# Loading the first q and v in head halves, and the first weights in row halves, in a fused attention and FFN kernel

## The chip, the cores and the metric

The kernel runs on one core of a Trainium2 chip. The metric is device time in microseconds (us), of one execution of the whole program; a time is the median of several executions. A "landing" is the moment at which the last of the sixteen parts of a transfer reports; landing times of single transfers were read from the trace's semaphore updates.

## The reference

Linear attention (softmax of q over the head dimension, of k over the sequence), then a gated FFN, for 8 batches of 576 rows, 8 heads of 64, and 512 → 1536 → 512 columns:

```python
q_s = softmax(q, axis=-1); k_s = softmax(k, axis=2)          # [8, 8, 576, 64] each
kv  = np.einsum('bhsd,bhse->bhde', k_s, v)
x   = np.einsum('bhsd,bhde->bhse', q_s, kv)                  # then to [4608, 512]
out = (gelu(x @ w_gate) * (x @ w_val)) @ w_out
```

## The kernel before

All matmuls are in fp16 and inputs arrive in f32, so every input passes through an exp or a cast. Batch 0's attention has to be done before the FFN can start; until then TensorE runs warm-up matmuls that nobody reads. Every load is issued by SyncE, in this order: q, k, v of batch 0, then the weights by column chunks. One call of `load` is two transfers, for the even and the odd SBUF rows:

```python
    WCH = [0, 128, 256] + list(range(512, F + 1, 256))     # weight column chunks
    wstp = ctx.enter_context(tc.tile_pool(name="wstp", bufs=6))   # staging buffers
    def load(src, nm, b, h0, h1, n0):
        tiles[(nm, b)] = ld_b[nm][b % len(ld_b[nm])]
        for t, c0 in ((0, n0), (1, 1)):
            nc.sync.dma_start(
                out=tiles[(nm, b)][t:P:2, h0:h1, c0 * D:NC * D],
                in_=src[b, h0:h1].rearrange("h (m n) d -> m h (n d)", n=NT)[...])
    # ... cut ...
    for src, nm, n0 in ((q, "q", 1), (k, "k", 0), (v, "v", 0)):
        load(src, nm, 0, 0, H, n0)
    for c in range(NW):
        load_w_gv(c)                       # one gate and one value chunk
    # ... cut ...
    exp("q", 0, 0, 4, 1); exp("q", 0, 4, 8, 1)        # ScalarE
    exp("k", 0, 0, 4);    exp("k", 0, 4, 8)
    warm_pe(35)
    norm(0, 0, "dve", 1); norm(0, 1, "pool", 1)       # head pairs 0 to 3
    norm(0, 2, "dve", 1); norm(0, 3, "pool", 1)
    unit_t(0, 0, "dve")                               # transposes of q, copy on VectorE
    warm_pe(9)
    cast_v(0, 0, 4, "dve"); cast_v(0, 4, 6, "act")
    unit_t(0, 1, "act")
    cast_v(0, 6, 8, "dve")
    # ... cut: loads of batches 1 and 2 ...
    warm_pe(2)
    unit_kv(0, 0); unit_kv(0, 1)                      # k^T v, lower and upper heads
    # ... cut: x, then ffn_first over two column tiles ...
```

The softmax here doesn't subtract the row's maximum and nothing guards it: scores larger than these inputs give would overflow.

Of the kernel before, what the change touches and what calls it, by code (L numbers as in the profile page):

```python
# [9 lines left out]
f32 = mybir.dt.float32  # L10
f16 = mybir.dt.float16
# [7 lines left out]
def kernel(  # L19
# [10 lines left out]
    nc = tc.nc  # L30
# [15 lines left out]
    VW = D + 1  # L46
    WCH = [0, 128, 256] + list(range(512, F + 1, 256))
    NW = len(WCH) - 1
# [15 lines left out]
    warm = const.tile([P, 512], f16)  # L64
    nc.vector.memset(warm, 0.0)
    ident = const.tile([P, P], f16)
    make_identity(nc, ident)
    mask = const.tile([P, 2, D], f32)
    nc.vector.memset(mask, 0.0)
    nc.vector.memset(mask[0:64, 0, :], 1.0)  # L70
    nc.vector.memset(mask[64:128, 1, :], 1.0)
    tiny = const.tile([P, 80], f32)
    nc.vector.memset(tiny, 0.0)
    ek_b, eq_b, v16_b = [], [], []
    for i in range(2):
        ek_b.append(const.tile([P, NC, C], f16, name=f"ek{i}"))
        eq_b.append(const.tile([P, NC, C], f16, name=f"eq{i}"))
        v16_i = const.tile([P, NC, H, VW + 1], f16, name=f"v16_{i}")
        nc.gpsimd.memset(v16_i[:, :, :, D:D + 1], 1.0)
        v16_b.append(v16_i)  # L80
    xtr = const.tile([P, HP, B * REM], f16)
    q0r = const.tile([64, H, D], f32)
    eq0r = const.tile([P, C], f16)
    nc.vector.memset(eq0r[64:128, :], 1.0)

    ld_b = {}
    for nm, n, fill in (("k", 2, -1e30), ("v", 1, 0.0), ("q", 2, 0.0)):
        ld_b[nm] = []
        for i in range(n):
            t = const.tile([P, H, NC * D], f32, name=f"{nm}t{i}")  # L90
            (nc.vector if i == 0 else nc.gpsimd).memset(t[:, :, 0:D], fill)
            ld_b[nm].append(t)

# [30 lines left out]
    def copy_on(eng, dst, src):  # L124
        if eng == "pool":
            nc.gpsimd.tensor_copy(out=dst, in_=src)  # L126
        elif eng == "act":
            nc.scalar.copy(out=dst, in_=src)  # L128
        else:
            nc.vector.tensor_copy(out=dst, in_=src)  # L130

    def cast_w(nm, c, eng="pool"):
# [42 lines left out]
    def norm(b, hp, eng="dve", n0=0):  # L175
        norm_sum(b, hp, n0)
        norm_mul(b, hp, eng)
# [41 lines left out]
    def unit_t(b, g, eng="dve"):  # L219
        eqt = get_eqt(b)  # L220
        pst = ps_att.tile([P, 2, MAIN], f16, name="pst", tag="att")
        for j in range(2):
            hp = 2 * g + j
            for n in range(NM):
                nc.tensor.transpose(  # L225
                    pst[:, j, n * P:(n + 1) * P],
                    eq_b[b % 2][:, n + 1, hp * P:(hp + 1) * P], ident)
        copy_on(eng, eqt[:, 2 * g:2 * g + 2, 0:MAIN], pst)

# [56 lines left out]
    def unit_xrem(b, eng="act"):  # L286
# [4 lines left out]
        copy_on(eng, xtr[:, :, b * REM:(b + 1) * REM], psx)  # L291

    def warm_pe(n):
        ps = ps_big.tile([P, 512], f32, name="pswarm", tag="mm")
        for _ in range(n):
            nc.tensor.matmul(ps, ident, warm, start=True, stop=True)  # L296
# [25 lines left out]
    def ffn_first(xt, after):  # L322
# [14 lines left out]
        for fi, (psg, psv) in enumerate(ps):  # L337
            mm_gv(psg, wg_sb, xt, fi, [3])
            mm_gv(psv, wv_sb, xt, fi, [3])
            hts.append(gate(psg, psv))  # L340
        return hts

# [61 lines left out]

    for src, nm, n0 in ((q, "q", 1), (k, "k", 0), (v, "v", 0)):
        load(src, nm, 0, 0, H, n0)
    for c in range(NW):
        load_w_gv(c)
    for c in range(3):
        load_w_o(c)  # L410
    load(q, "q", 1, 0, H, 0)
    for c in range(3, NO):
# [8 lines left out]
    exp("q", 0, 4, 8, 1)  # L421
    exp("k", 0, 0, 4)
    exp("k", 0, 4, 8)
    warm_pe(35)
    norm(0, 0, "dve", 1)
    norm(0, 1, "pool", 1)
    norm(0, 2, "dve", 1)
    norm(0, 3, "pool", 1)
    unit_t(0, 0, "dve")
    warm_pe(9)  # L430
    cast_v(0, 0, 4, "dve")
    cast_v(0, 4, 6, "act")
    unit_t(0, 1, "act")
    cast_v(0, 6, 8, "dve")
    for h0 in (0, 4):
# [3 lines left out]
    nc.sync.dma_start(out=q0r, in_=q[0].rearrange("h (m n) d -> m h (n d)", n=NT)[:, :, 0:D])  # L439
    warm_pe(2)  # L440
    unit_kv(0, 0)
    unit_kv(0, 1)
    cast_w("wg", 0, "pool")
    cast_w("wv", 0, "pool")
    unit_x(0, 0, "act", True)
    unit_x(0, 1, "act", True)
    unit_x(0, 2, "dve", True)
    unit_x(0, 3, "act", True)
    preload(ACTF.Gelu)
    for c in range(1, NW):  # L450
        cast_w("wg", c)
        cast_w("wv", c)
# [7 lines left out]
    def at(b, kind, i, *fns):  # L460
# [3 lines left out]

    at(0, FI, NFI - 1, L(exp, "q", 1), L(exp, "k", 1, 0, 4),
       L(cast_w_o, 3), L(cast_w_o, 4), L(cast_w_o, 5),
       L(norm, 1, 0), L(norm, 1, 1, "pool"), L(norm_sum, 1, 2), L(norm_mul, 1, 2, "pool"),
       L(cast_v, 1, 0, 4, "act"), L(exp, "k", 1, 4, 8))
# [6 lines left out]
              [L(unit_x, 1, 3, "dve")]]  # L475
    first = {0: [[], []], 1: first1}

# [53 lines left out]
    for b in order:  # L531
        xt = get_xt(b) if b < B else xtr
        hts = []
        fi0 = 0
        if b in first:
            hts = ffn_first(xt, first[b])
            fi0 = len(hts)
            ride(b, FI, fi0 - 1)
# [57 lines left out]
```

## Time and profile before

| | before |
|---|---|
| time, median | 321.69 us |
| span of the profiled execution | 319.8 us |
| q landed (two transfers) | 5.09, 6.35 |
| k landed | 8.17, 9.96 |
| v landed | 11.61, 12.93 |
| first kv matmul | 14.60 |
| first gate matmul of the FFN | 17.20 |
| third gate tile | 20.78 |

Read it from below. From the third gate tile on TensorE works at a fixed pace, so a microsecond there is a microsecond of the whole. It is late because a chain of transfers and element-wise work comes first. The lines of the profile that show this are in the prediction.

### The profile page before, as it was taken

To read this page: it belongs to the slowest core of one execution; us is meant where nothing else is said; L and a number is where in the kernel's file an instruction comes from. 1 tells how busy PE (TensorE), PEld (TensorE's weight loads), DVE (VectorE), ACT (ScalarE), POOL (GpSimd) and SP (SyncE) were. 2 spreads that over 40 slices of the span, in tenths; PEclk is the share of its full clock that TensorE was granted. 3 is DMA by queue.
4 is the path that set the end of the run, shared out by engine and by line. 5 is a ranking of instruction groups with operands and counts; after the bars stand their busy time and mean duration, and the time that the engine had idled before them with its cause. 6 is when DMAs were issued, how large, how long until landed. Compare 5 with 4: busy or idle time off the path is not lost.

```text
span 319.8 us, 4482 instructions
## 1 busy us (share of the span) xinstructions
PE 314.4 (98%) x1650; PEld 149.5 (47%) x1650; DVE 194.7 (61%) x343; ACT 140.0 (44%) x178; POOL 44.5 (14%) x60
## 2 busy tenths in 40 slices
PE   8999999999999999999999999999999999999995
PEld 3544454445445444544444444444444444444443
DVE  3944366498889578846794679457952444233431
ACT  3563564898352563246423743384321233103300
POOL 2567460340002000120003000300000000000000
PEclk9999999999999999999999999999999999999999
DMA  6999999940187216821492039302011110040002
GB/s 230 367 383 395 400 389 385 394 148 0 68 291 250 54 66 210 321 62 66 124 383 81 29 124 373 121 21 119 14 55 29 68 66 0 16 108 10 0 34 99
DMA packets 42342, 50.76 MB, mean 159 GB/s; under 512 B 3408, under 2 KB 38096, under 8 KB 42320
## 3 DMA queue, kind: packets, MB, share of 16 engines
q1 hardware_dynamic: 42176, 50.41, 45.6%
q8 instruction: 13, 0.21, 0.3%
q14 instruction: 9, 0.07, 0.1%
q10 hardware_dynamic: 144, 0.07, 0.1%
HBM read 37.75 MB, written 9.44 MB: 148 GB/s over the span
## 4 chain that ended last, share of the span: by engine, by line
PE 96%; ACT 1%; issue 1%; DVE 1%; POOL 0%; POOLq 0%; ACTq 0%
PE psg L304 28%; PE psy L348 28%; PE psv L304 28%; PE pswarm L296 4%; PE pskv L199 3%; PE psx L282 2%; PE pst L225 1%; PE psl L369 1%; DVE kv_sb L207 0%; ACT L309 0%; ACT L148 0%; PE psxr L289 0%; ACT eq L148 0%; PE pstr L237 0%; ACT gl L309 0%
## 5 line engine op out<-in xcount | busy, mean ns | idle before, releaser
L309 ACT ACTIVATE gl<-psg 128x512 f32<-128x512 f32 x108 | 63.9, 598 | 127.3 <-PE psg L304 125.5
L311 DVE SCALAR_TENSOR_TENSOR ht<-psv,gl 128x512 f16<-128x512 f32 x108 | 72.9, 682 | 64.7 <-PE psv L304 63.2
L304 PE MATMUL psg<-xt,wg_sb 128*128 128x512 f16 x384 | 100.6, 379 | 0.2
L304 PE MATMUL psv<-xt,wv_sb 128*128 128x512 f16 x384 | 100.2, 379 | 0.0
L348 PE MATMUL psy<-wo_sb,ht 128*128 128x512 f16 x420 | 95.5, 379 | 0.0
L304 PEld LDWEIGHTS <-wv_sb 128*128 128x128 f16 x432 | 42.2, 98 | 51.5 <-issue 0.9
L304 PEld LDWEIGHTS <-wg_sb 128*128 128x128 f16 x432 | 41.5, 98 | 47.6 <-issue 0.8
L348 PEld LDWEIGHTS <-ht 128*128 128x128 f16 x420 | 40.4, 98 | 47.2 <-DVE ht L311 0.2
L397 DVE TENSOR_SCALAR yo<-psy 128x512 f32<-128x512 f32 x30 | 20.6, 689 | 31.0 <-PE psy L348 31.0
L126 POOL CAST v<-vt 128x640 f16<-128x640 f32 x26 | 18.3, 743 | 140.1 <-DMA vt<-in_v_dram 122.9
L165 DVE TENSOR_REDUCE rq<-eq 128x10 f32<-128x640 f16 (+1 forms) x32 | 25.4, 792 | 9.3 <-ACT eq L148 8.9
L172 DVE TENSOR_TENSOR eq<-eq,rrq 128x640 f16<-128x640 f16 (+1 forms) x28 | 22.9, 817 | 0.3
L148 ACT ACTIVATE ek<-kt 128x1280 f16<-128x1280 f32 (+1 forms) x11 | 19.1, 1746 | 3.0 <-DVE rrq L167 1.6
L148 ACT ACTIVATE eq<-qt 128x2560 f16<-128x2560 f32 (+1 forms) x9 | 18.3, 2049 | 4.3 <-DMA qt<-in_q_dram 4.2
L248 DVE STREAM_TRANSPOSE et<-eq 128x640 f16<-128x640 f16 x20 | 16.9, 845 | 0.7
L128 ACT CAST xt<-psx 128x512 f16<-128x512 f32 x17 | 9.2, 588 | 15.9 <-PE psx L282 15.9
L296 PE MATMUL pswarm<-warm,ident 128*128 128x512 f16 x46 | 12.3, 430 | 1.4 <-POOL ident masks.py:199 1.4
L304 PE MATMUL psg<-xtr,wg_sb 128*128 128x512 f16 x48 | 12.3, 379 | 0.0
L304 PE MATMUL psv<-xtr,wv_sb 128*128 128x512 f16 x48 | 12.3, 379 | 0.0
L199 PEld LDWEIGHTS <-ek 128*128 128x128 f16 x160 | 10.3, 97 | 3.6 <-issue 0.4
L199 PE MATMUL pskv<-v,ek 128*128 128x130 f16 x160 | 11.8, 220 | 0.0
L130 DVE CAST xt<-psx 128x512 f16<-128x512 f32 x15 | 9.7, 682 | 1.8 <-PE psx L282 1.8
(59 smaller groups left out, 129.4 us busy)
## 6 DMA issues: line engine op xcount, KB each, us to landing
out_dram<-yo SPq DMA_DIRECT2D x14, 512.0 KB, 3.5
qt<-in_q_dram SPq DMA_DIRECT2D x9, 512.0 KB, 6.7
kt<-in_k_dram SPq DMA_DIRECT2D x7, 640.0 KB, 7.4
vt<-in_v_dram SPq DMA_DIRECT2D x7, 640.0 KB, 7.9
qt<-in_q_dram SPq DMA_DIRECT2D x7, 640.0 KB, 6.1
kt<-in_k_dram SPq DMA_DIRECT2D x7, 512.0 KB, 8.0
vt<-in_v_dram SPq DMA_DIRECT2D x7, 512.0 KB, 8.5
eqt<-et SPq DMA_DIRECT2D x80, 40.0 KB, 1.9
```

The costliest lines, as they stand in the source:

```text
L126: nc.gpsimd.tensor_copy(out=dst, in_=src)
L148: nc.scalar.activation(out=dst[:, n0:NC, h0 * D:h1 * D].rearrange("p n (h d) -> p h n d", d=D), in_=tiles[(nm, b)][:, h0:h1, n0 * D:NC * D ...
L165: nc.vector.reduce_sum(rq, e, axis=mybir.AxisListType.X)
L172: (nc.gpsimd if eng == "pool" else nc.vector).tensor_tensor(out=e, in0=e, in1=rrq.unsqueeze(-1).to_broadcast((P, n, 2, D)), op=ALU.mult)
L199: nc.tensor.matmul(pskv[:, j, :], ek_b[b % 2][:, n, hp * P:(hp + 1) * P], v16_b[b % 2][:, n, 2 * hp:2 * hp + 2, 0:VW], start=(n == 0), sto ...
L248: nc.vector.transpose(out=et[:, :, hp].rearrange("p c (n i) -> p n c i", i=32), in_=eq_b[b % 2][:, :, hp * P:(hp + 1) * P].rearrange("p n ...
L296: nc.tensor.matmul(ps, ident, warm, start=True, stop=True)
L304: nc.tensor.matmul(ps, w[:, ci, fi * P:(fi + 1) * P], xt[:, ci, :], start=(ci == 0), stop=(ci == HP - 1))
L309: nc.scalar.activation(out=gl, in_=psg, func=ACTF.Gelu)
L311: nc.vector.scalar_tensor_tensor(out=ht, in0=psv, scalar=_H_SCALE, in1=gl, op0=ALU.mult, op1=ALU.mult)
L348: nc.tensor.matmul(psy, hts[fi][:, ns * P:(ns + 1) * P], wo_sb[:, fi, :], start=(fi == 0), stop=(fi == NFI - 1))
L397: nc.vector.tensor_scalar(out=yo, in0=psy, scalar1=1.0 / _H_SCALE, scalar2=None, op0=ALU.mult)
```

## The change

The intent is to start that chain on half of the data. q and v come in head halves, so that the lower four heads are complete earlier; the first 256 weight columns come in row halves, as the lower rows are all that the lower heads' x needs; and the first two column tiles of gate and value run on the lower half while kv and x of the upper heads are still being made. Around it VectorE takes one multiply from GpSimd, ScalarE takes the first transpose copy ahead of k's exp, GpSimd takes the cast of v's last two heads from VectorE, VectorE takes the second transpose copy from ScalarE, and the memsets that k's and v's loads wait for go first. Cut to its core:

```diff
-    WCH = [0, 128, 256] + list(range(512, F + 1, 256))
+    WCH = [256, 384, 512] + list(range(768, F + 1, 256))
+    def load_w_rows(half):          # 256 columns, half of the rows; a staging tile per transfer
+        for w, nm in ((moe_w_gate, "wg"), (moe_w_val, "wv")):
+            t = wst_tile(f"{nm}st", 2, WCH[0])
+            nc.sync.dma_start(out=t, in_=...[:, 2 * half:2 * half + 2, 0:WCH[0]])
-    for src, nm, n0 in ((q, "q", 1), (k, "k", 0), (v, "v", 0)):
-        load(src, nm, 0, 0, H, n0)
+    load(q, "q", 0, 0, 4, 1)
+    load(q, "q", 0, 4, 8, 1)
+    load(k, "k", 0, 0, H, 0)
+    load(v, "v", 0, 0, 4, 0)
+    load(v, "v", 0, 4, 8, 0)
+    for half in range(2):
+        load_w_rows(half)
...
-    norm(0, 3, "pool", 1)
-    unit_t(0, 0, "dve")
+    norm(0, 3, "dve", 1)
+    unit_t(0, 0, "act")             # ahead of k's exps
+    exp("k", 0, 0, 4)
+    exp("k", 0, 4, 8)
...
     unit_kv(0, 0)
+    unit_x(0, 0, "dve", True)
+    unit_x(0, 1, "act", True)
+    unit_kv(0, 1)                   # ffn_first0 then runs two tiles on the lower half first
```

Cut: the order of memsets, the `ffn_first0` function, one warm-up bank for all warm-ups, q of batch 1 in two halves and one of its multiplies on VectorE.

More of the change, by code (lines that the diff above doesn't have):

```diff
@@ L64 @@
     warm = const.tile([P, 512], f16)
-    nc.vector.memset(warm, 0.0)
     ident = const.tile([P, P], f16)
-    make_identity(nc, ident)
     mask = const.tile([P, 2, D], f32)
-    nc.vector.memset(mask, 0.0)
-    nc.vector.memset(mask[0:64, 0, :], 1.0)
-    nc.vector.memset(mask[64:128, 1, :], 1.0)
     tiny = const.tile([P, 80], f32)
-    nc.vector.memset(tiny, 0.0)
     ek_b, eq_b, v16_b = [], [], []
@@ L77 @@
         eq_b.append(const.tile([P, NC, C], f16, name=f"eq{i}"))
-        v16_i = const.tile([P, NC, H, VW + 1], f16, name=f"v16_{i}")
-        nc.gpsimd.memset(v16_i[:, :, :, D:D + 1], 1.0)
-        v16_b.append(v16_i)
+        v16_b.append(const.tile([P, NC, H, VW + 1], f16, name=f"v16_{i}"))
     xtr = const.tile([P, HP, B * REM], f16)
@@ L83 @@
     eq0r = const.tile([P, C], f16)
-    nc.vector.memset(eq0r[64:128, :], 1.0)
-    ld_b = {}
-    for nm, n, fill in (("k", 2, -1e30), ("v", 1, 0.0), ("q", 2, 0.0)):
-        ld_b[nm] = []
-        for i in range(n):
-            t = const.tile([P, H, NC * D], f32, name=f"{nm}t{i}")
-            (nc.vector if i == 0 else nc.gpsimd).memset(t[:, :, 0:D], fill)
-            ld_b[nm].append(t)
+    ld_b = {nm: [const.tile([P, H, NC * D], f32, name=f"{nm}t{i}") for i in range(n)]
+            for nm, n in (("k", 2), ("v", 1), ("q", 2))}
+    nc.vector.memset(warm, 0.0)
+    nc.vector.memset(ld_b["k"][0][:, :, 0:D], -1e30)
+    nc.vector.memset(ld_b["v"][0][:, :, 0:D], 0.0)
+    nc.vector.memset(tiny, 0.0)
+    nc.vector.memset(mask, 0.0)
+    nc.vector.memset(mask[0:64, 0, :], 1.0)
+    nc.vector.memset(mask[64:128, 1, :], 1.0)
+    nc.vector.memset(eq0r[64:128, :], 1.0)
+    nc.vector.memset(ld_b["q"][0][:, :, 0:D], 0.0)
+    make_identity(nc, ident)
+    for i in range(2):
+        nc.gpsimd.memset(v16_b[i][:, :, :, D:D + 1], 1.0)
+    nc.gpsimd.memset(ld_b["k"][1][:, :, 0:D], -1e30)
+    nc.gpsimd.memset(ld_b["q"][1][:, :, 0:D], 0.0)
     wg_sb = wpool.tile([P, HP, F], f16, name="wg_sb")
@@ L130, in copy_on, with cast_w_rows @@
             nc.vector.tensor_copy(out=dst, in_=src)
+    def load_w_rows(half):
+        for w, nm in ((moe_w_gate, "wg"), (moe_w_val, "wv")):
+            t = wst_tile(f"{nm}st", 2, WCH[0])
+            nc.sync.dma_start(
+                out=t, in_=w.rearrange("(ci p) f -> p ci f", p=P)[
+                    :, 2 * half:2 * half + 2, 0:WCH[0]])
+            wst[(nm, "rows", half)] = t
+    def cast_w_rows(nm, half, eng="pool"):
+        dst = (wg_sb if nm == "wg" else wv_sb)[:, 2 * half:2 * half + 2, 0:WCH[0]]
+        copy_on(eng, dst, wst[(nm, "rows", half)])
     def cast_w(nm, c, eng="pool"):
@@ L227, in unit_t @@
                     eq_b[b % 2][:, n + 1, hp * P:(hp + 1) * P], ident)
-        copy_on(eng, eqt[:, 2 * g:2 * g + 2, 0:MAIN], pst)
+        st["evac_t"] = lambda eng: copy_on(eng, eqt[:, 2 * g:2 * g + 2, 0:MAIN], pst)
+        if eng != "none":
+            st["evac_t"](eng)
     def unit_trem(b):
@@ L291, in unit_xrem @@
         copy_on(eng, xtr[:, :, b * REM:(b + 1) * REM], psx)
+    pswarm = ps_big.tile([P, 512], f32, name="pswarm", tag="mm")
     def warm_pe(n):
-        ps = ps_big.tile([P, 512], f32, name="pswarm", tag="mm")
+        ps = pswarm
         for _ in range(n):
@@ L340, in ffn_first, with ffn_first0 @@
             hts.append(gate(psg, psv))
+        return hts
+    def ffn_first0(xt, after):
+        ps = {}
+        for fi in range(2):
+            for nm in ("g", "v"):
+                ps[(nm, fi)] = ps_big.tile([P, 512], f32, name="ps" + nm, tag="mm")
+        for nm, w in (("g", wg_sb), ("v", wv_sb)):
+            for ci in range(2):
+                for fi in range(2):
+                    mm_gv(ps[(nm, fi)], w, xt, fi, [ci])
+            after.pop(0)()
+        for nm, w in (("g", wg_sb), ("v", wv_sb)):
+            for fi in range(2):
+                mm_gv(ps[(nm, fi)], w, xt, fi, [2])
+        hts = []
+        for fi in range(2):
+            for nm, w in (("g", wg_sb), ("v", wv_sb)):
+                mm_gv(ps[(nm, fi)], w, xt, fi, [3])
+            hts.append(gate(ps[("g", fi)], ps[("v", fi)]))
         return hts
@@ L410 @@
         load_w_o(c)
-    load(q, "q", 1, 0, H, 0)
+    load(q, "q", 1, 0, 4, 0)
+    load(q, "q", 1, 4, 8, 0)
     for c in range(3, NO):
@@ L421 @@
     exp("q", 0, 4, 8, 1)
-    exp("k", 0, 0, 4)
-    exp("k", 0, 4, 8)
-    warm_pe(35)
     norm(0, 0, "dve", 1)
@@ L427 @@
     norm(0, 2, "dve", 1)
-    norm(0, 3, "pool", 1)
-    unit_t(0, 0, "dve")
-    warm_pe(9)
+    norm(0, 3, "dve", 1)
+    warm_pe(29)
+    unit_t(0, 0, "act")
+    exp("k", 0, 0, 4)
+    exp("k", 0, 4, 8)
+    warm_pe(8)
+    unit_t(0, 1, "none")
     cast_v(0, 0, 4, "dve")
+    st["evac_t"]("dve")
     cast_v(0, 4, 6, "act")
-    unit_t(0, 1, "act")
-    cast_v(0, 6, 8, "dve")
+    cast_v(0, 6, 8, "pool")
+    warm_pe(2)
+    for half in range(2):
+        cast_w_rows("wg", half)
+        cast_w_rows("wv", half)
+    unit_kv(0, 0)
+    warm_pe(2)
+    unit_x(0, 0, "dve", True)
+    unit_x(0, 1, "act", True)
+    warm_pe(1)
+    unit_kv(0, 1)
+    preload(ACTF.Gelu)
     for h0 in (0, 4):
@@ L439 @@
     nc.sync.dma_start(out=q0r, in_=q[0].rearrange("h (m n) d -> m h (n d)", n=NT)[:, :, 0:D])
-    warm_pe(2)
-    unit_kv(0, 0)
-    unit_kv(0, 1)
-    cast_w("wg", 0, "pool")
-    cast_w("wv", 0, "pool")
-    unit_x(0, 0, "act", True)
-    unit_x(0, 1, "act", True)
-    unit_x(0, 2, "dve", True)
-    unit_x(0, 3, "act", True)
-    preload(ACTF.Gelu)
-    for c in range(1, NW):
+    for c in range(NW):
         cast_w("wg", c)
@@ L463 @@
     L = lambda f, *a: (lambda: f(*a))
-    at(0, FI, NFI - 1, L(exp, "q", 1), L(exp, "k", 1, 0, 4),
+    at(0, FI, NFI - 1, L(exp, "q", 1, 0, 4), L(exp, "q", 1, 4, 8), L(exp, "k", 1, 0, 4),
        L(cast_w_o, 3), L(cast_w_o, 4), L(cast_w_o, 5),
-       L(norm, 1, 0), L(norm, 1, 1, "pool"), L(norm_sum, 1, 2), L(norm_mul, 1, 2, "pool"),
+       L(norm, 1, 0), L(norm, 1, 1), L(norm_sum, 1, 2), L(norm_mul, 1, 2, "pool"),
        L(cast_v, 1, 0, 4, "act"), L(exp, "k", 1, 4, 8))
@@ L475 @@
               [L(unit_x, 1, 3, "dve")]]
-    first = {0: [[], []], 1: first1}
+    first0 = [L(unit_x, 0, 2, "act"), L(unit_x, 0, 3, "dve")]
     at(1, FI, 2, L(unit_trem, 1))
@@ L534 @@
         fi0 = 0
-        if b in first:
-            hts = ffn_first(xt, first[b])
+        if b < 2:
+            hts = ffn_first0(xt, first0) if b == 0 else ffn_first(xt, first1)
             fi0 = len(hts)
```

## The prediction

> **What bounds the kernel now.** I read the page's busy table and clock row first, then the chain of waits, then the timeline of each engine over the first 21 us, because the change touches only the start.
>
> ```profile
> PE 314.4 (98%) x1650; PEld 149.5 (47%) x1650; DVE 194.7 (61%) x343; ACT 140.0 (44%) x178; POOL 44.5 (14%) x60
> PEclk9999999999999999999999999999999999999999
> PE 96%; ACT 1%; issue 1%; DVE 1%; POOL 0%; POOLq 0%; ACTq 0%
> ```
>
> TensorE is busy for 98% of the span, at full granted clock, and is 96% of the chain that ended last. But part of that is warm-up, matmuls whose result nobody reads. The timeline of TensorE shows which:
>
> ```profile
> 1.36 9.65 PE L296 MATMUL pswarm<-warm,ident 128*128 128x512 f16 x35 [1.36 <-POOL ident masks.py:199]
> 10.85 0.82 PE L225 MATMUL pst<-ident,eq 128*128 128x128 f16 x8
> 11.50 2.10 PE L296 MATMUL pswarm<-warm,ident 128*128 128x512 f16 x9
> 13.44 0.79 PE L225 MATMUL pst<-ident,eq 128*128 128x128 f16 x8
> 14.07 0.59 PE L296 MATMUL pswarm<-warm,ident 128*128 128x512 f16 x2
> 14.60 1.46 PE L199 MATMUL pskv<-v,ek 128*128 128x130 f16 x20
> 15.99 1.37 PE L282 MATMUL psx<-eqt,kv_sb 128*128 128x512 f16 x4
> 17.20 0.72 PE L304 MATMUL psg<-xt,wg_sb 128*128 128x512 f16 x2
> 20.78 1.03 PE L304 MATMUL psg<-xt,wg_sb 128*128 128x512 f16 x4
> 21.64 1.03 PE L304 MATMUL psv<-xt,wv_sb 128*128 128x512 f16 x4
> ```
>
> The kv matmuls start at 14.60, the first gate matmul at 17.20, the third gate tile (column tile 2) at 20.78, and from there four matmuls take 21.64 - 20.78 = 0.86 us, again and again. So 20.78 is the mark to watch: all that follows is TensorE work at a fixed pace, and the end moves with it. From 20.78 on I find, in the starts of successive matmuls, 1.4 us of pauses in all, most of them at the seam to batch 1 (46 to 65 us) and each behind work that TensorE itself released. The gain can only be what the start gives. What sets 14.60 and 17.20 is in the timelines of the other engines (VectorE, ScalarE, GpSimd in this order):
>
> ```profile
> 7.53 0.69 DVE L165 TENSOR_REDUCE rq<-eq 128x8 f32<-128x512 f16 x1 [3.35 <-ACT eq L148]
> 10.84 0.92 DVE L172 TENSOR_TENSOR eq<-eq,rrq 128x512 f16<-128x512 f16 x1
> 12.51 0.64 DVE L130 COPY eqt<-pst 128x1024 f16<-128x1024 f16 x1
> 13.06 2.21 DVE L130 CAST v<-vt 128x1280 f16<-128x1280 f32 x2
> 15.38 0.17 DVE L204 RECIPROCAL rck<-pskv 128x2 f32<-128x2 f32 x1
> 6.44 2.00 ACT L148 ACTIVATE eq<-qt 128x1024 f16<-128x1024 f32 x2 [4.20 <-DMA qt<-in_q_dram]
> 10.07 2.43 ACT L148 ACTIVATE ek<-kt 128x1280 f16<-128x1280 f32 x2 [1.63 <-DVE rrq L167]
> 12.73 1.04 POOL L172 TENSOR_TENSOR eq<-eq,rrq 128x512 f16<-128x512 f16 x1 [1.52 <-DVE rrq L167]
> 13.74 1.18 POOL L126 CAST wg_sb<-wgst 128x512 f16<-128x512 f32 x1
> 15.69 0.61 POOL L126 CAST wg_sb<-wgst 128x512 f16<-128x512 f32 x1
> ```
>
> ScalarE waits for q until 6.44, VectorE starts on its first sum at 7.53 and is then occupied without a gap until after 15. It is the path: q, exp, norms, one transpose copy, v casts, kv. Single transfers' landing times in the trace: q 5.09 and 6.35, k 8.17 and 9.96, v 11.61 and 12.93, the first weight chunks 13.69 (gate) and 14.49 (value).
>
> **What the Trainium skill says.** "TensorE: Matmul & The Clock Gate", section "Back-to-back issue gap", gives N / 2.4 + 2.5 ns for a warm matmul, 216 ns at 512 columns; the trace agrees (0.86 us for four). "GPSIMD Engine Reference", section "1. Specifications", says that GpSimd's SBUF interfaces are shared with VectorE, with contention against VectorE instructions in a two-port mode or with two SBUF inputs. The trace agrees: the cast at 13.74, beside the v cast, took 1.18 us and the same form at 15.69 took 0.61; the two-input multiply on VectorE at 10.84, beside GpSimd's multiply at 10.17, took 0.92 where the earlier one at 8.48, with GpSimd idle, took 0.69. "VectorE: DVE Perf Modes", section "Mode 2×_2P — use both read ports for one tensor", lets a single-source SBUF copy run at two elements per cycle, f32 included. No uncontended cast of v is in this trace; I come back to it. "DMA: Bandwidth & Descriptors", section "Specifications", asks for at least 512 B for line rate. Here both the 512 B weight rows and the 1 KB rows arrive at 344 to 395 GB/s, so I expect little from the longer rows.
>
> **The change part by part.** The bytes ahead of any given point are unchanged: q, k, v, then 1 MB of weights (row halves of 256 columns in place of two 128-column chunks), so the DMA stream, which is saturated, gives nothing. Only what has to have landed before work starts is smaller.
>
> 1. q in head halves. The lower heads are complete when half of q is, about 5.2 (half the bytes by the first landing of 5.09), against 6.35. The first exp takes half of 2.00, 1.04 with its start. So VectorE's first sum starts at about 5.3 + 1.04 + 0.05 = 6.4, not 7.53: 1.1 us earlier.
>
> 2. Norms. VectorE now multiplies for pairs 0, 2 and 3; GpSimd keeps pair 1. Step by step (sum 0.69, reciprocal 0.20, multiply 0.69, all from the rows before, starts overlapping a little): sum 0 6.4, multiply 0 7.35 to 8.05, sum 1 to 8.65, reciprocal to 8.85, sum 2 to 9.4, multiply 2 (beside GpSimd, 0.92) to 10.6, sum 3 to 11.2, multiply 3 to 12.15. Before, the last sum ended at 12.35 and GpSimd's multiply at 13.77; so the fourth pair is 1.6 us earlier though VectorE does one multiply more.
>
> 3. The first transpose copy moves to ScalarE (a 128x1024 copy there took 1.01 at 14.27) ahead of k's exp. TensorE is ready after 29 warm-ups at about 9.5, GpSimd's multiply ends near 10.0, so the copy runs 10.45 to 11.5, the k exps to 12.75 and 14.0, the v cast of heads 4, 5 to 14.75. Before, the k exps were done at 12.50. This is later but the lower half needs only 12.75.
>
> 4. Casting the lower v. Half of v has landed at about 11.45 (9.96 plus half of the 2.97 to 12.93), VectorE is free at 12.2. The cast of 128x1280 took 1.40 before with GpSimd beside it all the time. Now GpSimd stands still until v's upper half lands at 12.95. At one element per cycle it would again take 1.4 (sum rows of 640 take 0.82, of 512 take 0.69, which puts the fixed part at 0.17, and 1280 at 1.5); that it took less, contended, suggests the double rate, which is 0.67 + 0.17 = 0.84. So the lower kv matmuls start between 13.2 and 13.75, not at 14.60.
>
> 5. From kv to the third tile. Before, kv start to first x was 15.99 - 14.60 = 1.39 us (ten matmuls, reciprocal, the masked multiply). Then: x 0 and 1 at 14.6 and 14.85 (fast cast) or 15.1 and 15.4 (slow), the copies of x take 0.43 to begin and 0.69, so x tile 0 is in SBUF at 15.7 or 16.2. Meanwhile one warm-up and the upper kv (0.65) end at 15.95 or 16.45. The gate matmuls start there. Before it was 17.20, but two x matmuls (2 x 0.216 = 0.43) now stand behind that point. From there 18 matmuls x 0.216 = 3.89 and 0.1 for the last copy of x (ended at about 0.1 after the ci 2 matmuls) give 19.9 or 20.45 for the third tile, against 20.78.
>
> 6. Weights. GpSimd casts the row halves from about 13.8 on, 0.61 to 0.65 each: ready at 14.6, 15.2, 15.9 and 16.5, each ahead of its use (15.95, 17.0, and 18.1 for the lower rows' gate, value, and the upper rows). The third tile's chunk lands at about 16.5 and 17.3 and is cast by 18. No stall.
>
> Sum: 0.33 (slow cast) to 0.88 us (fast cast). Fewer warm-ups (42 for 46) save nothing by themselves, as they only fill waits. Batch 1: q in halves lets VectorE start its norms 1.2 us earlier and pays back the multiply moved from GpSimd (0.82); pauses there are behind TensorE's own kv and x, and I expect them unchanged.
>
> **The rivals.** (a) The path moves to ScalarE: its copy before k's exp delays the upper k exp and v cast to 14.75. For it: ScalarE has no gap from 10.45 on. Against: the upper kv is not reached before 15.3. If the copy were 1 us later the gain falls to about zero, 321.7. (b) Weights bind: the upper row halves or their casts come late because SP waits for a free staging buffer, of which there are six. For it: SP waited for GpSimd casts before, 3.3 us in total for the value chunks. Against: at least 1 MB stays in flight. It would cost some 0.5 us, 321.7 or more. (c) The gain is eaten at batch 1's seam, where k and v land at fixed times (42.59 to 47.15, DMA-bound). Against: kv of batch 1 came at 47.63, a microsecond and more after its data; 321.5 at worst. (d) Everything arrives as in the fast cast and a pause at the seam shrinks as well: 320.6.
>
> **Range and chances.** I take the middle of 0.33 and 0.88, slightly towards the fast cast: 0.65 off 321.69, so 321.0 us. The runs before scatter over 0.56; with the rivals the range is 320.2 to 321.8. Two per cent would be 6.4 us, ten times what the start offers and far over any cost named, so faster or slower by that much gets 0.01 each.
>
> **What would show it.** Right: the first sum near 6.4, multiply 3 ended near 12.2, lower kv at 13.2 to 13.8, first gate matmul near 16.2, third tile near 20.2, and then the same pace and the same pauses. The duration of the lower v cast on VectorE decides between 0.84 and 1.4. Wrong: a lower-half q that lands near 6, a first gate matmul that waits for GpSimd's casts, a pause of over 0.2 us before the ci 2 or ci 3 matmuls, or a new pause near 46 to 54 us.

## The result, and the profile after

The changed kernel took 324.19 us (323.71 to 324.69, four runs), the kernel before 321.82 us in the same rounds (321.52 to 322.08). The ratio is 1.0074, with a 95% interval of 1.0056 to 1.0092. Ratios here are the mean time of one kernel's fast runs over that of the other's fast runs of the same rounds, so not quite the ratio of the quoted medians. It is within 2%, as predicted, but slower, and outside the predicted range.

The page's busy table and chain, of the changed kernel:

```profile
span 321.6 us, 4488 instructions
PE 312.9 (97%) x1646; PEld 148.8 (46%) x1646; DVE 196.3 (61%) x345; ACT 139.7 (43%) x178; POOL 42.9 (13%) x61
PE 88%; DMA 6%; ACT 1%; DVE 1%; issue 1%; POOL 1%; ACTq 0%
```

TensorE was 96% of the chain, is 88% now, and transfers have come in with 6%. The chain followed back from the early part of the span (start, duration, what) says which:

```profile
3.57 7.96 DMA kt<-in_k_dram
```

Eight microseconds from the issue of k's first transfer to its landing at 11.53; in the kernel before it was five (3.12 to 8.17). The timelines of the changed kernel (start, duration, engine, line, operation; in brackets the idle time before it and what ended that) confirm it on each engine:

```profile
9.12 0.69 DVE L178 TENSOR_REDUCE rq<-eq 128x8 f32<-128x512 f16 x1 [0.67 <-ACT eq L161]
14.52 0.83 DVE L130 CAST v<-vt 128x1280 f16<-128x1280 f32 x1 [2.19 <-DMA vt<-in_v_dram]
...
12.95 2.43 ACT L161 ACTIVATE ek<-kt 128x1280 f16<-128x1280 f32 x2 [1.80 <-DMA kt<-in_k_dram]
...
15.49 0.73 PE L212 MATMUL pskv<-v,ek 128*128 128x130 f16 x10 [2.28 <-ACT ek L161]
22.12 1.03 PE L321 MATMUL psg<-xt,wg_sb 128*128 128x512 f16 x4
26.93 1.04 PE L321 MATMUL psv<-xt,wv_sb 128*128 128x512 f16 x4 [0.33 <-POOL wv_sb L126]
```

VectorE is no longer occupied without a gap: it waits 0.67 us for the upper q and 2.19 us for the lower v. ScalarE waits 1.80 us for k. The bracket of the kv matmuls names k's second exp, which ended at 15.38; the cast of the lower v ended at 15.35, and it is the one that decides, as in a run below ("q halves by two engines") kv starts at 12.78, right after its cast, with k's second exp done only at 13.47. The third gate tile starts at 22.12, 1.34 us later than before. At 26.93 there is a second, separate loss: TensorE waits for GpSimd's cast of weights; in the starts of successive matmuls this pause is 0.49 us. 1.34 + 0.49 = 1.83 us, and the spans differ by 321.6 - 319.8 = 1.8 us. That is nearly the whole difference: one more new pause, of 0.16 us at 46.09, stands against 0.21 us less of waiting in the transposes of batches 1 and 2.

No byte has been added. So look at the transfers themselves. Windows of one microsecond (stretch, its length, then PE, PEld, DVE, ACT, POOL with counts, clock, mean busy share of the DMA engines, which passes 1 where packets overlap, and GB/s), the kernel before:

```profile
5.00:6.00 1.00, 1.00 (x5) 0.45 (x4) 0.00 (x0) 0.00 (x0) 0.00 (x0) 1.00 1.08 378
6.00:7.00 1.00, 1.00 (x7) 0.43 (x5) 0.00 (x0) 0.56 (x1) 0.00 (x0) 1.00 1.04 379
...
18.00:19.00 1.00, 1.00 (x6) 0.46 (x5) 0.00 (x0) 1.00 (x1) 0.62 (x2) 1.00 1.08 382
```

and the changed kernel:

```profile
5.00:6.00 1.00, 1.00 (x6) 0.43 (x5) 0.04 (x1) 0.93 (x1) 0.00 (x0) 1.00 0.76 215
6.00:7.00 1.00, 1.00 (x6) 0.49 (x5) 0.93 (x3) 0.00 (x0) 0.00 (x0) 1.00 0.74 195
...
18.00:19.00 1.00, 1.00 (x10) 0.48 (x8) 0.61 (x3) 0.98 (x2) 0.93 (x2) 1.00 0.52 147
```

There are two holes in a stream that the prediction called saturated, one at 4 to 10 us and one at 17 to 19 us. SyncE's own timeline, with GpSimd's first cast of weights, explains the second at once; changed kernel:

```profile
14.44 0.37 SPq L120 DMA_DIRECT2D wvst<-in_moe_w_val_dram  x1
17.32 0.37 SPq L120 DMA_DIRECT2D wgst<-in_moe_w_gate_dram  x1
...
16.68 0.61 POOL L126 CAST wg_sb<-wgst 128x512 f16<-128x512 f32 x1
```

After the issue at 14.44 SyncE issues nothing until 17.32: the six staging buffers are taken, four of them by the four row transfers, until GpSimd has cast the first, and GpSimd casts late because v came late (its first weight cast starts at 16.68, and at 13.74 in the kernel before). The first four weight transfers took four buffers in the kernel before as well, but the next two held 512 KB each, and here 256 KB, so 1.5 MB is under way in place of 2 MB. For the first hole, compare the issues in both kernels. Before, then changed:

```profile
3.12 1.28 SPq L104 DMA_DIRECT2D kt<-in_k_dram  x2
```

```profile
1.57 1.96 SPq L104 DMA_DIRECT2D qt<-in_q_dram  x3
```

One issue takes 1.28 / 2 = 0.64 us for transfers of 640 and 512 KB, and 1.96 / 3 = 0.65 us for transfers of 256 KB: the same for half the bytes. A 256 KB transfer per 0.65 us is 262,144 B / 0.65 us = 403 GB/s, hardly over the 360 to 388 GB/s at which the full stream drains. At the head of the stream nothing is queued yet, and so nothing piles up. That was my suspicion at this point, against the rival that short transfers lose as such, whoever issues them; the experiments settle a part of it.

### The profile page after: what moved, and what is told of

Its sections match the earlier page's. It is cut to its first block, busy times and chain, and to the rows that moved or that the text cites. A ratio compares the mean times of both kernels' runs of the same rounds, so it can differ in the third digit from the quotient of the medians.

```text
span 321.6 us, 4488 instructions
## 1 busy us (share of the span) xinstructions
PE 312.9 (97%) x1646; PEld 148.8 (46%) x1646; DVE 196.3 (61%) x345; ACT 139.7 (43%) x178; POOL 42.9 (13%) x61
## 4 chain that ended last, share of the span: by engine, by line
PE 88%; DMA 6%; ACT 1%; DVE 1%; issue 1%; POOL 1%; ACTq 0%
PE psy L386 28%; PE psg L321 27%; PE psv L321 27%; PE pskv L212 3%; DMA kt<-in_k_dram 2%; DMA wvst<-in_moe_w_val_dram 2%; DMA wgst<-in_moe_w_gate_dram 2%; PE psx L297 2%; PE psl L407 1%; POOL wv_sb L126 1%; PE pst L238 0%; ACT L326 0%; ACT L161 0%; PE psxr L304 0%; ACT eq L161 0%
## 5 line engine op out<-in xcount | busy, mean ns | idle before, releaser
L126 POOL CAST v<-vt 128x640 f16<-128x640 f32 x27 | 19.0, 743 | 145.9 <-DMA vt<-in_v_dram 97.8
L185 DVE TENSOR_TENSOR eq<-eq,rrq 128x640 f16<-128x640 f16 (+1 forms) x30 | 24.8, 826 | 0.5 <-DVE rrq L180 0.2
L161 ACT ACTIVATE eq<-qt 128x2560 f16<-128x2560 f32 (+2 forms) x10 | 18.6, 1865 | 4.5 <-DMA qt<-in_q_dram 4.4
L212 PEld LDWEIGHTS <-ek 128*128 128x128 f16 x160 | 10.4, 97 | 6.0 <-ACT ek L161 2.7
L313 PE MATMUL pswarm<-warm,ident 128*128 128x512 f16 x42 | 11.3, 419 | 1.4 <-POOL ident masks.py:199 1.4
L130 DVE CAST xt<-psx 128x512 f16<-128x512 f32 x16 | 10.4, 683 | 3.1 <-PE psx L297 3.1
```

The lines of the kernel that those rows point to most:

```text
L126: nc.gpsimd.tensor_copy(out=dst, in_=src)
L161: nc.scalar.activation(out=dst[:, n0:NC, h0 * D:h1 * D].rearrange("p n (h d) -> p h n d", d=D), in_=tiles[(nm, b)][:, h0:h1, n0 * D:NC * D ...
L185: (nc.gpsimd if eng == "pool" else nc.vector).tensor_tensor(out=e, in0=e, in1=rrq.unsqueeze(-1).to_broadcast((P, n, 2, D)), op=ALU.mult)
L212: nc.tensor.matmul(pskv[:, j, :], ek_b[b % 2][:, n, hp * P:(hp + 1) * P], v16_b[b % 2][:, n, 2 * hp:2 * hp + 2, 0:VW], start=(n == 0), sto ...
L313: nc.tensor.matmul(ps, ident, warm, start=True, stop=True)
```

## The experiments

All ran correct. "Third tile" is the start of the third gate tile in the profiled run, "pauses" those of TensorE behind weight casts after it. Each ratio is to the runs of the kernel before in the same rounds (medians 321.77 to 322.27). Three more runs are told in the text alone.

| run | ratio (95%) | median us | k landed | lower kv | third tile | pauses |
|---|---|---|---|---|---|---|
| before | 1 | 321.82 | 9.96 | 14.60 | 20.78 | none |
| changed | 1.0074 (1.0056 to 1.0092) | 324.19 | 12.86 | 15.49 | 22.12 | 0.49 |
| changed, q whole | 1.0014 (0.9995 to 1.0033) | 322.41 | 10.69 | 14.29 | 20.92 | 0.50, 0.44 |
| changed, v whole | 1.0126 (1.0090 to 1.0162) | 325.54 | 12.36 | 16.44 | 24.49 | none |
| changed, q and v whole | 1.0004 (0.9989 to 1.0019) | 322.16 | 10.86 | 14.91 | 21.54 | none |
| before, q in head halves | 1.0063 (1.0034 to 1.0092) | 323.95 | 11.46 | 15.60 | 21.77 | none |
| before, q in row quarters | 1.0034 (1.0019 to 1.0049) | 323.44 | 12.03 | 16.41 | 22.58 | none |
| changed, upper q by ScalarE | 0.9986 (0.9963 to 1.0009) | 321.98 | 10.57 | 14.23 | 20.86 | 0.28, 0.35 |
| changed, rows in two tiles | 1.0038 (1.0006 to 1.0070) | 323.88 | 12.13 | 14.77 | 21.39 | 0.11, 0.40 |
| changed, q whole, rows in two tiles | 1.0002 (0.9986 to 1.0019) | 322.57 | 10.22 | 14.94 | 21.56 | none |
| before, long q issued slowly | 1.0064 (1.0052 to 1.0076) | 323.96 | 10.30 | 15.55 | 21.72 | none |
| changed, q halves by two engines | 0.9982 (0.9970 to 0.9994) | 321.36 | 10.14 | 12.78 | 19.40 | 0.60, 0.46 |
| the same, rows in two tiles | 0.9963 (0.9950 to 0.9977) | 320.65 | 10.46 | 13.10 | 19.72 | 0.19 |
| reordered, q whole | 0.9974 (0.9957 to 0.9991) | 321.29 | 10.23 | 13.57 | 20.41 | none |
| reordered, q halves by two engines | 0.9976 (0.9961 to 0.9990) | 320.99 | 10.45 | 12.99 | 19.65 | none |

### Which part costs: undoing the halves, and doing them alone

Four kernels. Three undo the halves of q, of v, or of both in the changed kernel; the fourth has only q's halves in the kernel before.

```diff
 # changed, q whole                     # changed, v whole
-    load(q, "q", 0, 0, 4, 1)           -    load(v, "v", 0, 0, 4, 0)
-    load(q, "q", 0, 4, 8, 1)           -    load(v, "v", 0, 4, 8, 0)
+    load(q, "q", 0, 0, H, 1)           +    load(v, "v", 0, 0, H, 0)
```

> The changed kernel with q of batch 0 loaded whole (two transfers) again, all else as changed. Theory 1 (the four short q transfers upset the stream of transfers between 4 and 10 us, so that one or two of the 16 queues run 2 to 3 us late): k lands again near 10.0 and lower v near 11.5, the spread from the first to the last sixteenth of k falls from 3.3 us to under 1, and the time to 320.9 to 321.9. Rival 2 (the number of transfers, v's halves as much as q's): a part of the spread stays, 322.5 to 323.5. Rival 3 (not the loads but the work of the other engines): landings and 324.2 stay.

> The changed kernel with v of batch 0 whole again, q in halves. Theory 1: k still lands at 11.5 and 12.9 and the time stays 324 or gets worse, 324.2 to 325. Rival 2: k's landing improves or, as v comes after it, v's spread at least; 322.5 to 323.5. Rival 3: 324.2.

> The changed kernel with q and v whole again. Theory 1: stream as in the kernel before (v at 12.9), time 321.5 to 322.3: the order of work costs or gains little by itself. Rival 3: 324.

> The kernel before with q of batch 0 in head halves and nothing else changed. Theory 1: k and v land 2 to 3 us later, time 323 to 324.5. Rival 2: 322 to 323. Rival 3: as before or a little faster, 321.3 to 321.9.

With q whole the ratio falls from 1.0074 to 1.0014, and k lands at 10.69 rather than 12.86. With q's halves alone in the kernel before, the ratio is 1.0063. q's halves are the cause of most of the loss, undone and done alone. Not of all of it: with q whole I had expected k near 10.0, its sixteen parts within 1 us and 321.9 us at most, and it was 10.69, 1.60 and 322.41. Their window of 5 to 6 us, changed kernel with q whole:

```profile
5.00:6.00 1.00, 1.00 (x6) 0.42 (x5) 0.00 (x0) 0.00 (x0) 0.00 (x0) 1.00 1.09 364
```

and kernel before with q in halves:

```profile
5.00:6.00 1.00, 1.00 (x3) 0.30 (x2) 0.09 (x1) 0.88 (x1) 0.00 (x0) 1.00 0.84 186
```

I find no cost of v's halves: undone alone they make it worse (1.0126), as k is still late and the lower kv now waits for all of v (15.37). This run shows something else too. TensorE was mostly idle from 13.4 to 16.4 us, and its clock was then halved in the window of 18.0 to 20.8 us (the value ahead of the last two):

```profile
18.00:20.80 2.80, 2.80 (x15) 1.80 (x15) 1.07 (x4) 1.87 (x2) 2.65 (x5) 0.50 0.83 238
```

So a part of its 1.0126 is clock, and its third tile at 24.49 isn't to be read as waiting alone. With both whole the ratio is 1.0004 and nothing pauses, but nothing is won either.

### Is it the head-half shape? Row quarters, and weights first

One kernel splits q into the same number of transfers by rows in place of heads; the other keeps the head halves but lets 1 MB of weights go in front of them.

```diff
 # before, q in row quarters: four transfers of 32 SBUF rows, all heads
+    for m0 in (0, 32):
+        for t in (0, 1):
+            nc.sync.dma_start(out=ld_b["q"][0][2 * m0 + t:2 * m0 + 64:2, :, D:NC * D], in_=...)
 # before, weights first
+    load_w_gv(0)
+    load_w_gv(1)
+    load(q, "q", 0, 0, 4, 1)
+    load(q, "q", 0, 4, 8, 1)
```

> The kernel before with q of batch 0 in four transfers of 256 KB again, but cut by rows (32 partitions with all 8 heads each) instead of by heads. Theory 1a (starved by issue: four issues of 256 KB at 0.65 us each barely keep up with 385 GB/s, so queues run dry between 5 and 7 us and drift apart): the same dip, k landed after 11, time 323 to 324.5. Rival 1b (the shape: a head half touches other addresses): no dip, k landed by 10.2, time 321.5 to 322.2.

> The kernel before with 1 MB of weights (the two 128-column chunks) issued first and q in head halves behind it; slower by construction, only its stream of transfers is looked at. By v's last landing the same bytes have moved as by the second value chunk's landing, 15.99, in the kernel before. Theory 1a (short transfers dry the queues out only while nothing stands in front of them): no dip, last v at 15.7 to 16.4, the mean busy share of the queues never under 1.0 between 5 and 12 us. Rival 1b (a head half as such is slow): a dip when q's halves pass at about 6 to 9 us, last v after 17.3.

Row quarters are slower than the kernel before as well (1.0034), but in another way: the queues are busy all the time (share 1.08 to 1.13) and move only 211 to 255 GB/s, as a packet of 1 KB takes 69 to 87 ns on average (4 to 7 us) in place of 46. Four transfers of 32 rows each are slow packet by packet, which the head halves are not, so this run, though its time and k's landing fell where the first theory had them, says nothing about the number of transfers. The other run says more, but it is a single execution (325.5 us, its state unknown). Its windows:

```profile
4.00:5.00 1.00, 1.00 (x5) 0.38 (x4) 0.17 (x1) 0.00 (x0) 0.00 (x0) 1.00 0.77 185
5.00:6.00 1.00, 1.00 (x7) 0.41 (x6) 0.00 (x0) 0.00 (x0) 0.00 (x0) 1.00 0.77 224
6.00:7.00 1.00, 1.00 (x6) 0.48 (x5) 0.00 (x0) 0.00 (x0) 0.00 (x0) 1.00 1.03 337
```

The hole at 4 to 6 us stays, where the theory had no share under 1.0, though now weights pass there, and from 6 us on, with q's halves passing, the stream is full. In this execution it is the place at the head of the stream that loses, not q and not its shape. But these weights were issued every 0.53 us (495 GB/s) and still left a hole, so 403 GB/s against the drain rate cannot be all of it.

### Who issues, and how fast

The first kernel lets ScalarE issue the upper half of q while SyncE issues the lower. The second splits each half over the two engines, so that the lower half still comes first. The third is the opposite test in the kernel before: the transfers stay long, but a transfer of 64 bytes after each of q's two costs SyncE another half microsecond.

```diff
 # changed, upper q by ScalarE
+    load(q, "q", 0, 4, 8, 1, nc.scalar)
 # changed, q halves by two engines
-            nc.sync.dma_start(
+            (engs or (nc.sync, nc.sync))[t].dma_start(         # t: even rows, odd rows
+    load(q, "q", 0, 0, 4, 1, (nc.sync, nc.scalar))
+    load(q, "q", 0, 4, 8, 1, (nc.sync, nc.scalar))
 # before, long q issued slowly
+            if nm == "q":
+                nc.sync.dma_start(out=idle_t[:, t, :], in_=q[0, 0, 0:1, 0:16])
```

> The changed kernel with the upper heads of q issued by ScalarE's queue while SP issues the lower heads, so that q is issued in 1.3 instead of 2.6 us. Theory 1a: no dip, k lands near 10, lower v near 11.6, and the order of work shows its gain of 0.3 to 0.9 less what the staging buffers cost (theory 2): 321.0 to 322.4. Rival 1b: dip stays, 323.5 to 325.

> The changed kernel with each head half of q issued by two engines: its even rows by SyncE, its odd rows by ScalarE, at the same time. The order of lower before upper stays, the transfers stay at 256 KB, but 512 KB are handed out per 0.65 us. Theory (issue-bound): DMA share 1.0 or more from 4 to 8 us, lower q by 4.9, upper q by 6.6, k by 10.4 (9.96 before, 12.86 in the changed kernel), lower kv at 13.6 to 14.3, third gate tile at 20.3 to 20.9, plus the weight pauses of up to 0.5 us; ratio to the kernel before 0.997 to 1.000. Rival (short transfers lose whoever issues them): share under 0.9 somewhere in 5 to 8 us, k after 11.5, third tile after 21.5, ratio 1.004 to 1.008.

> The kernel before with a 64-byte transfer issued after each of q's two 512 KB transfers, so that SyncE hands out 512 KB per some 1.2 us in place of 512 KB per 0.65 us at the head of the stream, with no transfer shortened. Theory (issue-bound: SyncE takes about 0.65 us for a transfer whatever its size, 256 KB per 0.65 us is 403 GB/s, no more than the queues drain, so no backlog builds and every irregularity empties a queue): DMA share under 0.95 and under 340 GB/s somewhere in 4 to 7 us, k landed at 10.4 to 11.2 rather than 9.96, third gate tile at 21.0 to 21.6, ratio 1.001 to 1.004. Rival (the shortness of the transfers themselves): share stays at 1.03 or more, k lands within 0.3 us of 9.96 plus what it is issued later, third tile at 20.8, ratio 1.000.

The second is the decisive run. The transfers are as short as in the changed kernel and the lower half still comes first, but two engines issue them. Two things change with that: q is handed out in 1.65 us in place of 2.80, and half of it goes through a second DMA queue (q10 in the trace, next to q1).

```profile
5.00:6.00 1.00, 1.00 (x7) 0.41 (x6) 0.04 (x1) 0.93 (x1) 0.00 (x0) 1.00 1.05 369
6.00:7.00 1.00, 1.00 (x6) 0.47 (x5) 0.93 (x3) 0.65 (x1) 0.00 (x0) 1.00 1.05 339
```

The hole is gone, q lands at 4.79 and 6.26, k at 10.14 in place of 12.86, and the ratio goes from 1.0074 to 0.9982. Short transfers do not lose as such; whether the pace of the issue or the second queue is what helps, this run can't tell. Its timeline of TensorE shows what the change was meant to give, and what it still loses:

```profile
12.78 0.74 PE L212 MATMUL pskv<-v,ek 128*128 128x130 f16 x10
19.40 1.03 PE L321 MATMUL psg<-xt,wg_sb 128*128 128x512 f16 x4
23.45 1.04 PE L321 MATMUL psg<-xt,wg_sb 128*128 128x512 f16 x4 [0.43 <-POOL wg_sb L126]
24.79 1.04 PE L321 MATMUL psv<-xt,wv_sb 128*128 128x512 f16 x4 [0.30 <-POOL wv_sb L126]
```

The third tile is 20.78 - 19.40 = 1.38 us earlier than before, beyond what the sum promised, and 0.60 + 0.46 = 1.06 us of it go to waits for weights. Two more pauses (0.16 us at 44 and 0.38 us at 73) take the rest: the span of this profiled execution, the longest of the five, is 319.9 us, the same as before.

The first kernel repairs the stream as well (k at 10.57), but two queues at once interleave: lower and upper parts land at 4.31, 4.98, 5.71 and 6.39, so the first exp starts at 6.47, as late as before (6.44), and the point of the halves is lost. The third, slow issue of long transfers, costs 1.0064, as much as the halves do. Its windows thin out in the same place, though less than I expected:

```profile
4.00:5.00 1.00, 1.00 (x4) 0.35 (x3) 0.17 (x1) 0.00 (x0) 0.00 (x0) 1.00 0.98 298
5.00:6.00 1.00, 1.00 (x3) 0.30 (x2) 0.00 (x0) 0.00 (x0) 0.00 (x0) 1.00 1.00 308
```

The share was to be under 0.95 and k to land after 10.4; it is 0.98 and 10.30, while the third tile (21.72) and the ratio lie beyond what I had expected (21.6 and 1.004). Most of its loss is direct: the second half of q was issued later and landed at 7.29 in place of 6.35, and the third tile follows by the same 0.94 us; a pause of 0.60 us at 47 us, in the transposes of batch 1, comes on top. The thinner windows agree with the issue rate as the cause, but a share near 1 is not one of empty queues. The packets' own records show what fills it: of those that start from 4 to 6 us, 20 took over 0.1 us here (the longest 0.63 us) and 16 in the changed kernel (0.89 us, 22% of all packet time), against 2 with two engines and 2 in the kernel before; the median is 0.046 us in all four. So a hole is in part empty queues and in part single packets that hang, and what makes these hang is not shown.

### The second hole: staging buffers

The row transfers get two staging tiles in place of four, each row half in its slice: in the changed kernel, with q whole, and with q's halves issued by two engines.

```diff
+            if half == 0:
+                wst[(nm, "both")] = wst_tile(f"{nm}st", HP, WCH[0])
-            t = wst_tile(f"{nm}st", 2, WCH[0])
+            t = wst[(nm, "both")][:, 2 * half:2 * half + 2, :]
```

> The changed kernel, q in halves, with the two row halves of each weight in one staging buffer, so that the four row transfers hold two buffers and not four. Theory 2 (four small transfers fill four of six buffers, so only 1.5 MB is under way, SP waits for casts until 17.3 and the stream dries up from 17 to 23 us, which costs the 0.49 us pause of TensorE at 26.9): SP issues the 384-column chunk before 16, the rate stays over 340 GB/s from 17 to 23, no pause at 26 to 27; time 0.4 to 0.6 less than the changed kernel, 323.5 to 323.9. Rival: 324.2 as before, the pause comes from the late start of the weights.

> The changed kernel with q whole and the row halves in two staging buffers. Theories 1 and 2 together: neither dip, neither of the pauses at 24.9 and 26.2 us of the run with q whole alone (0.50 and 0.44 us); time 321.2 to 321.6, about 0.9 less than with q whole alone and a little under the kernel before. If theory 2 is wrong: 322.4.

> The changed kernel, its order of work untouched, with both faults mended: q's head halves issued by SyncE and ScalarE at once, and the four row transfers of the first 256 weight columns in two staging tiles, not four. Theory (these two account for the whole miss): lower kv at 12.7 to 13.0 and third gate tile at 19.3 to 19.7 as with two engines alone, no weight pause of over 0.15 us between 19 and 27 us (there it was 0.60 and 0.46), ratio to the kernel before 0.994 to 0.9965. Rival (with an earlier start the weights' own transfers bind, whatever the staging tiles): pauses of 0.5 us or more in all remain between 19 and 27 us, ratio 0.997 to 0.999.

In the changed kernel this alone is at most a partial repair: 1.0038, with an interval (1.0006 to 1.0070) that overlaps the one without it. SyncE issues on (the next chunk at 14.53), but the rate, which was to stay over 340 GB/s, still falls to 207 at 19 to 20 us, and pauses of 0.11 and 0.40 us stay, which I had expected to vanish. The first hole is still in this stream, and I take the lateness from there to be the reason, which is not shown. With q whole the pauses are gone, but the gain is not there (1.0002). The reason is a third effect, in the timelines of VectorE and GpSimd:

```profile
13.45 1.34 DVE L130 CAST v<-vt 128x1280 f16<-128x1280 f32 x1
...
13.38 0.73 POOL L126 CAST v<-vt 128x640 f16<-128x640 f32 x1 [1.95 <-DMA vt<-in_v_dram]
14.06 1.20 POOL L126 CAST wg_sb<-wgst 128x512 f16<-128x512 f32 x1
```

GpSimd's cast of the upper v now starts just before the lower v's cast on VectorE, which takes 1.34 us in place of 0.83, and kv waits. GpSimd's next cast takes 1.20 us in place of 0.61. With q early enough the two don't meet. So the third kernel is the one that counts: the changed kernel, its order of work untouched, with both holes mended. It took 320.65 us (320.58 to 321.19), the kernel before 322.17 us beside it: 0.9963 (0.9950 to 0.9977). Its TensorE timeline and a window:

```profile
13.10 0.73 PE L214 MATMUL pskv<-v,ek 128*128 128x130 f16 x10 [0.29 <-DVE v L130]
19.72 1.03 PE L323 MATMUL psg<-xt,wg_sb 128*128 128x512 f16 x4
```

```profile
18.00:19.00 1.00, 1.00 (x6) 0.41 (x5) 0.69 (x1) 0.00 (x0) 0.87 (x2) 1.00 1.06 362
```

The stream at 18 us is full (1.06, not 0.52), and one pause of 0.19 us is left of 1.06, a little over the 0.15 that I had allowed. The lower kv at 13.10 and the third tile at 19.72 lie just past the expected 13.0 and 19.7. The two places account for the miss: the kernel that lost 0.7% gains 0.4% with them mended.

### A reordered kernel

Before I knew of the two engines I built on q whole, with rows in two tiles, and moved work: k's first exp ahead of the copy on ScalarE, the cast of v ahead of the fourth multiply on VectorE, and the second transposes behind the lower kv, in place of four warm-ups. Three variants of it followed: k's memset late again, q as 512 + 256 + 256 KB, and q in halves issued by two engines.

```diff
 # reordered, q whole; on top of q whole and rows in two tiles
-    norm(0, 3, "dve", 1)
+    norm_sum(0, 3, 1)
-    unit_t(0, 0, "act")
     exp("k", 0, 0, 4)
+    unit_t(0, 0, "act")
     exp("k", 0, 4, 8)
     cast_v(0, 0, 4, "dve")
+    norm_mul(0, 3)
     unit_kv(0, 0)
+    unit_t(0, 1, "act")
```

> The changed kernel with q whole, the row halves in two staging buffers, k's first exp ahead of the transpose copy on ScalarE, the v cast ahead of the fourth multiply on VectorE, and the second transpose after the lower kv. Worked out from the runs with q whole: lower kv at 13.8 to 14.0 (VectorE's last reciprocal ends at 12.8, the cast 0.85, and 0.15), upper kv at 15.5, gate at 16.2, third tile at 20.3 to 20.6, no pauses from weights: 321.2 to 321.7 for a kernel before of 321.7 to 322.0, ratio 0.998 to 0.9995. If ScalarE's copies bind instead: third tile at 21 and ratio 1.000 to 1.002.

> The same with k's memset as late as in the kernel before, so that SP issues k at 3.1 and not at 2.2. If k's early issue right behind q is what gives the smaller dip at 6 us that all runs with q whole and the new order of memsets show (busy share 0.87 to 0.97 there, 1.04 in the kernel before; k spread over 1.2 to 1.9 us, not 0.4), it is gone here, k lands at 10.0 and the time is 0.1 to 0.4 under best1. If not: the same dip and time.

> The best version so far with q in three transfers: even rows whole (512 KB), then odd rows in head halves (256 KB each). The lower heads are complete at about 5.8 instead of 6.5 us. If the loss comes from short transfers at the head of the stream with nothing in front of them: the first 512 KB are front enough, no dip of the busy share under 0.95 from 4 to 6 us, k by 10.3, first sum at 6.9, third tile at 19.9 to 20.2 and a time 0.3 to 0.5 under the best version, ratio to the kernel before 0.995 to 0.997. If a short transfer loses time wherever it stands in the first 7 us: a dip of 0.75 to 0.9 at 5 to 8, k after 11, and a ratio of 0.999 to 1.003.

> The best kernel so far (q whole, row halves of the weights in two staging tiles, k's exp ahead of the copy) with q in head halves again, each half issued by SyncE and ScalarE at once. Theory (issue-bound): share 1.0 or more from 4 to 8 us, lower q by 4.9, k by 10.4, first sum near 6.2, lower kv at 12.9 to 13.5, third tile at 19.9 to 20.4, ratio to the kernel before 0.995 to 0.9975. Rival (short transfers lose): k after 11.5, lower kv after 14.0, third tile after 20.9, ratio 0.999 or more.

The reordered kernel reached 0.9974 (third tile 20.41, no weight pause). k's memset late gave 0.9979. The small dip that it was to cure became shallower (share 0.98 in place of 0.87 at 6 to 7 us), but k landed at 11.36 and not at 10.0; k's issue moved by only 0.66 us (2.25 to 2.91), and the test decides nothing. q in thirds gave 0.9988 and a third tile at 21.18, not 20.2: no dip under 0.95 from 4 to 6 us, but the last sixteenth of the third transfer landed at 8.73, 1.95 us behind the other fifteen, and k at 11.98. So 512 KB in front did not help here. With two engines, third tile at 19.65, it came to 0.9976, no better than 0.9974 within the intervals, though its third tile is 0.76 us earlier. One pause of 0.26 us came in at 43 us. The two profiled executions do differ by about what is left (spans of 319.3 and 318.7 us), but the six runs scatter from 320.45 to 321.73 us and hide it. Neither it nor the reordered kernel is told apart from the best one above (0.9963) by intervals alone, as they overlap.

## Why the prediction was wrong

The step that failed is the opening sentence of the part-by-part sum: "The bytes ahead of any given point are unchanged [...] so the DMA stream, which is saturated, gives nothing." Bytes were counted and issues weren't. Four transfers of q took SyncE 2.80 us where two took 1.47, and from 4 to 8 us the stream moved 195 to 299 GB/s, not the 361 to 388 of the kernel before. So step 4 took k's 9.96 unchanged and had the lower v landed at 11.45; k landed at 12.86 and the lower v at 14.42. That q's four transfers through SyncE at the head of the stream do this is shown by undoing them, by doing them alone and by the second engine. That it is the pace of the issue is argued: the second engine brings a second queue too, and weights at 495 GB/s left a hole. The table takes the steps in turn; the last column is the changed kernel with q issued by two engines, which differs in nothing else in the program.

| step | predicted | changed | two engines |
|---|---|---|---|
| 1. lower q landed; first sum | 5.2; 6.4 | 4.78; 5.96 | 4.79; 5.96 |
| 2. multiply 3 ended | 12.15 | 12.32 | 11.75 |
| 3. first copy on ScalarE | 10.45 to 11.5 | 10.13 to 11.14 | 10.13 to 11.14 |
| 3. k exps done | 14.0 | 15.38 | 13.47 |
| 4. lower v landed | 11.45 | 14.42 | 11.71 |
| 4. lower v cast | 0.84 | 0.83 | 0.83 |
| 4. lower kv starts | 13.2 to 13.75 | 15.49 | 12.78 |
| 5. from lower kv to third tile | 6.7 | 6.63 | 6.62 |
| 6. pauses for weights | none | 0.49 | 0.60, 0.46 |

Step 1 was right, and even modest. Steps 2 and 3 lost only what late data took: the upper q landed at 7.95 rather than 6.35, k at 12.86 rather than 9.96. Step 4's open question, whether f32 is cast at the double rate, came out as I guessed from the sums (0.83), as long as GpSimd is quiet (1.34 otherwise). Its landing time is the term that was off, by 3 us. Step 5 held to a tenth. Where the stream is kept full, the mechanism works as told, and the third tile comes even earlier than the sum said, at 19.40.

Of the rivals, (b) was real and I dismissed it: "at least 1 MB stays in flight" was true of the kernel before, but in the changed kernel SyncE, with four of six buffers held by row transfers, issued nothing for 2.5 us. So step 6's "No stall" failed too. The 0.5 us that I gave it is the 0.49 measured in the changed kernel, by luck: with the earlier start of two engines it was 1.06. It came on top of the first loss. Rival (a), ScalarE's copy, did not bind in the changed kernel: k came later than the copy ended (11.14), and with two engines kv started right after the cast of v. Rival (c) did not eat the gain: the larger pauses at the seam to batch 1 are the same in both kernels (0.17, 0.20, 0.36 and 0.25 us). One of 0.16 us at 46.09 is new, where the multiply of batch 1 that VectorE took over lasted 1.60 us beside a cast on GpSimd, and not 0.82. The rival that happened, transfers that arrive later because there are more of them, was not on my list.

What stays open: how much is the pace of the issue and how much the single queue, why some packets hang, why 256 KB transfers issued every 0.53 us still left a hole at the head of the stream, and why the sixteen parts of one transfer drift as far apart as they do (k's parts by 3.3 us in the changed kernel, by 0.4 us before).

## What to carry to other kernels

Splitting a load halves the bytes that the first consumer waits for, and here left the time of each issue as it was (0.65 us); at the start of a kernel, compare bytes per issue over the issue time with the drain rate, and if they are close, try two engines that issue the pieces in the order in which they are needed. When a transfer is split, count staging buffers in transfers, not in bytes. When a change to an overlapped start makes things slower, read the DMA share of the first microseconds in both kernels before looking at any engine.

## What the Trainium skill lacked or had wrong

- "DMA: Bandwidth & Descriptors", section "Rules for kernel authors", advises 128 partitions and 1 MiB or more per transfer for full bandwidth, and calls only those under 64 KB mostly overhead. It lacks the issue time: 0.65 us for a load of q whether it is 256 or 512 KB. Transfers of 256 KB did no harm in a full stream (337 GB/s and more from 6 us on with weights first, one execution), and at the head of an empty one they left it at 195 to 299 GB/s from 4 to 8 us, with k 2.9 us late.
- The same page, section "Issuing engines are not separate DMA queues", says that issuing from several engines saves only the sequencer's time, "usually small relative to the DMA itself", and the rules call spreading over engines no help for bandwidth. Here the two are equal: 0.65 us to issue, 0.67 to 0.73 us to move 256 KB at 360 to 394 GB/s. Issuing q from two engines took the ratio from 1.0074 to 0.9982.
- "TensorE: Matmul & The Clock Gate", section "Back-to-back issue gap", which the prediction cites for its 216 ns, calls that the gap of an isolated matmul and gives about 131 ns for 512 columns in a stream of weight loads and matmuls. Here such a stream ran at 0.86 / 4 = 0.215 us for each matmul.
